# State products on half-array tiles: 128x64 tiles side by side in place of one full-array product

## The chip, the cores and the metric

One core of a Trainium2 chip. The metric is the device time of one execution in microseconds (us). Most executions of one kernel agree within 0.3%; all runs compared below are of the fast state, except row_tiles, a single run whose state is unknown. The word "span" is the profiled execution from its first to its last instruction; it is about 1.8 us shorter than the device time. The "granted clock" is the share of full TensorE speed that the throttle let through; 1.0 is all of it. The "chain of waits" is the chain of work that ended last, followed back from the last instruction to whatever released it.

## The reference

Linear attention without a softmax, then a feed-forward block. Cut to what matters:

```python
# batch 8, heads 8, seq 576, head_dim 64
kv  = np.einsum('bhsd,bhse->bhde', k, v)      # the state: one 64x64 matrix per head  <- this change
out = np.einsum('bhsd,bhde->bhse', q, kv)
out = out / rms(out) * g_norm
x   = out.transpose(0, 2, 1, 3).reshape(4608, 512)
xn  = x / rms(x) * rms_g
y   = (silu(xn @ w_gate) * (xn @ w_val)) @ w_out     # 512 -> 1536 -> 512, nearly all of the work
```

## The kernel before

The kernel runs the feed-forward block of batch n in 12 "up" units (four gate and four value matmuls of 512 columns each) and 4 "down" units, and places the attention work of batch n+1 between them. The state of batch n+1 is made after units 0 and 1 (that of batch 2 after units 2 and 3). Batches 0 and 1 are loaded in another layout and already use 64x64 tiles; batches 2 to 7 take the second half of `kv_pair`, which is what the change touches. There, one matmul serves two heads: 128 columns of weights from k (two heads) and 128 moving columns from v (the same two heads). Its result is a 128x128 block of which only the two 64x64 blocks on the diagonal are used.

```python
    def kv_pair(ps, b, j, first, last):
        if b < EARLY:                      # batches 0 and 1: 64x64 tiles
            ...
            return
        hs = slice(2 * j, 2 * j + 2)
        for t in range(T + 1):             # 5 chunks of rows
            PE.matmul(
                ps, lhsT=bufs[b]["k"][:, t, hs, :], rhs=bufs[b]["v"][:, t, hs, :],
                start=(first and t == 0), stop=(last and t == T),
            )
    ...
        def kv_products(self, js):
            if js[0] == 0:
                self.kv_ps = att_pool.tile([128, NS, 128], FP32, name="att_ps")
            for j in js:
                kv_pair(self.kv_ps[:, j, :], self.n, j, j == 0, j == NS - 1)

        def kv_copy(self):                 # only the diagonal blocks are copied out
            n, ps = self.n, self.kv_ps
            SC.copy(out=kv_all[0:D, n, :, 0:D], in_=ps[0:D, :, 0:D])
            DVE.tensor_copy(out=kv_all[D:128, n, :, D:128], in_=ps[D:128, :, D:128])
    ...
            kv0, os = (2, (4, 5, 7, 8)) if n == 1 else (0, (2, 3, 5, 6))
            if not a.tail:                 # placed after two successive up units
                steps[kv0] += [lambda a=a: a.kv_products((0, 1))]
                steps[kv0 + 1] += [lambda a=a: a.kv_products((2, 3)), a.kv_copy]
            for c, u in enumerate(os):     # first product that reads the state: unit 2
                steps[u].append(lambda a=a, c=c: a.o(c))
```

So there are 12 "groups" of state products (6 batches, two each), every group 10 matmuls between full-array matmuls of 512 columns. One other place uses column tiles already: the products of the sequence tails (`o_products`, line L338), four groups of 8 matmuls of 128x64 weights and 128 moving columns, alternating between the left and the right half of the array.

Of the kernel before, what the change touches and what calls it, by code (L numbers as in the profile page):

```python
# [20 lines left out]
def kernel(  # L21
# [14 lines left out]
    B, H, S, D = q.shape  # L36
# [5 lines left out]
    T = 4  # L42
# [35 lines left out]
    PE, DVE, SC, GP = nc.tensor, nc.vector, nc.scalar, nc.gpsimd  # L78
# [34 lines left out]
    bufs = {b: {"k": kbs[b % 2], "v": vbs[b % 2]} for b in range(B)}  # L113
# [8 lines left out]
    def pairs_buf(b, name):  # L122
        flat = bufs[b][name].rearrange("p t h d -> p (t h d)")
        return flat[:, 0 : NS * C * D].rearrange("p (j c d) -> p j c d", j=NS, c=C)
# [135 lines left out]
    def kv_pair(ps, b, j, first, last):  # L260
        if b < EARLY:
            for c in range(C):
                for u in range(2):
                    rows = slice(u * D, u * D + D)
                    PE.matmul(  # L265
                        ps[rows, rows], lhsT=pairs_buf(b, "k")[rows, j, c, :], rhs=pairs_buf(b, "v")[rows, j, c, :],
                        start=(first and c == 0), stop=(last and c == C - 1),
                    )
            return
        hs = slice(2 * j, 2 * j + 2)  # L270
        for t in range(T + 1):
            PE.matmul(  # L272
                ps, lhsT=bufs[b]["k"][:, t, hs, :], rhs=bufs[b]["v"][:, t, hs, :],
                start=(first and t == 0), stop=(last and t == T),
            )

    def clear_tail_rows(i, engine):

# [12 lines left out]
    class Att:  # L291
# [8 lines left out]
# [5 lines that stand above are left out]
# [345 lines left out]
    def state0(j, dummies):  # L650
        ps = att_pool.tile([128, 512], FP32, name="att_ps")
        warm(ps, max(dummies, 1), 512 if dummies else 128)
        kv_pair(ps[:, 0:128], 0, j, True, True)
        return ps
# [101 lines left out]
    first = ffn.pair_banks()  # L756
# [202 lines left out]
    for n in range(1, B + 1):  # L959
# [25 lines left out]
        b = n + 2  # L985
# [53 lines left out]
```

## Time and profile before

| | before |
|---|---|
| time, median (first runs) | 324.66 us (324.35 to 336.14) |
| span of the profiled run | 322.7 us, granted clock 1.0 |
| TensorE busy | 98% of the span |
| chain of waits | 92% TensorE |
| state products of batches 2 to 7 | 120 matmuls in 12 groups, 0.559 us each, 6.7 us in all |

The page of the kernel before, busy time and chain of waits (time, share of the span, number of instructions; then the shares of the chain by engine; then two groups of instructions, with busy us, mean ns of one, and us idle before them; PE is TensorE's matmuls, PEld its weight loads):

```profile
span 322.7 us, 5143 instructions
...
PE 316.0 (98%) x1925; PEld 156.5 (49%) x1925; DVE 181.5 (56%) x373; ACT 178.3 (55%) x318; POOL 20.3 (6%) x42
...
PE 92%; DMA 4%; DVE 2%; SPq 0%; ACT 0%; issue 0%; DVEq 0%
...
L272 PEld LDWEIGHTS <-kb 128*128 128x128 bf16 x120 | 7.7, 98 | 2.8
L272 PE MATMUL att_ps<-vb,kb 128*128 128x128 bf16 x120 | 8.7, 219 | 0.0
```

A busy share near 100% does not prove a bound by itself, since a matmul's record (219 ns here) is longer than its pace. What proves it is the order in time. Here is TensorE around the two groups of batch 3 (start, time to the last end, instruction, count); only the starts are to be read, since ends overlap:

```profile
90.08 1.03 PE L472 MATMUL v_ps<-xnt,wv_sb 128*128 128x512 bf16 x4
90.94 0.72 PE L272 MATMUL att_ps<-vb,kb 128*128 128x128 bf16 x10
91.50 1.03 PE L472 MATMUL g_ps<-xnt,wg_sb 128*128 128x512 bf16 x4
92.36 1.03 PE L472 MATMUL v_ps<-xnt,wv_sb 128*128 128x512 bf16 x4
93.22 0.72 PE L272 MATMUL att_ps<-vb,kb 128*128 128x128 bf16 x10
```

Four matmuls of 512 columns take 0.86 us wherever they stand (90.08 to 90.94, 91.50 to 92.36), so nothing is lost on either side of a group, and the group takes 91.50 - 90.94 = 0.56 us, 56 ns a matmul. The column-tiled groups that the kernel already has look different:

```profile
258.98 1.03 PE L472 MATMUL v_ps<-xnt,wv_sb 128*128 128x512 bf16 x4
259.94 0.41 PE L338 MATMUL att_ps<-kv_all,qt 128*64 128x128 bf16 x8
260.28 1.04 PE L472 MATMUL g_ps<-xnt,wg_sb 128*128 128x512 bf16 x4
261.15 1.03 PE L472 MATMUL v_ps<-xnt,wv_sb 128*128 128x512 bf16 x4
```

Here the four matmuls ahead of the group take 0.96 us, not 0.86, and the group is longer than its pairs explain. These lines, and the 64x64 groups of batches 0 and 1, are what the prediction is built from.

### The profile page before, as it was taken

The numbers are of one execution on the slowest core, as the hardware profiler recorded it, in microseconds if no ns is written. First come the engines' busy times: TensorE is split into PE (matmuls) and PEld (weight loads), VectorE is DVE, ScalarE is ACT, GpSimd is POOL, SyncE is SP. The second block draws the span as 40 slices with busy tenths as digits, with TensorE's granted clock in tenths as the row PEclk, the third lists the DMA queues.
The fourth block names the chain that finished last, engine by engine and source line by source line (L and its number), as shares of the span: only waits on it lengthen the run. The fifth ranks groups of instructions, "written<-read, shape, count | busy, mean of one in ns | idle before, by whom it ended". The sixth has DMA issues, their size and how long they took to land.

```text
span 322.7 us, 5143 instructions
## 1 busy us (share of the span) xinstructions
PE 316.0 (98%) x1925; PEld 156.5 (49%) x1925; DVE 181.5 (56%) x373; ACT 178.3 (55%) x318; POOL 20.3 (6%) x42
## 2 busy tenths in 40 slices
PE   8899999999999999999999999999999999999995
PEld 3575456554455445544554454445544444444443
DVE  4785767568438922793279417850696068703310
ACT  3576447666757475747664766576554355223321
POOL 1363251100000000000000000000000000000000
PEclk9999999999999999999999999999999999999999
DMA  7999999887379557924792378936102600240014
GB/s 277 355 351 386 377 374 293 214 265 176 65 195 295 132 143 163 328 54 114 187 328 56 73 202 222 315 55 169 43 2 49 182 31 1 48 147 4 0 35 98
DMA packets 74421, 54.87 MB, mean 170 GB/s; under 512 B 42264, under 2 KB 67100, under 8 KB 74396
## 3 DMA queue, kind: packets, MB, share of 16 engines
q1 hardware_dynamic: 74016, 53.88, 58.4%
q10 hardware_dynamic: 380, 0.66, 0.6%
q8 instruction: 15, 0.25, 0.3%
q14 instruction: 10, 0.08, 0.1%
HBM read 37.75 MB, written 9.44 MB: 146 GB/s over the span
## 4 chain that ended last, share of the span: by engine, by line
PE 92%; DMA 4%; DVE 2%; SPq 0%; ACT 0%; issue 0%; DVEq 0%
PE g_ps L472 28%; PE v_ps L472 28%; PE o_ps L516 27%; DMA st<-in_q_dram 3%; PE att_ps L272 2%; PE att_ps L343 2%; PE v_ps L516 1%; PE g_ps L516 1%; DVE xna L453 1%; DMA out_dram<-o_sb 1%; PE v_ps L489 1%; PE o_ps L489 1%; PE g_ps L489 0%; PE att_ps L338 0%; PE att_ps L285 0%; PE att_ps L265 0%
## 5 line engine op out<-in xcount | busy, mean ns | idle before, releaser
L478 DVE TENSOR_TENSOR h_sb<-silu,v_ps 128x512 bf16<-128x512 bf16 x104 | 71.0, 683 | 110.3 <-ACT silu L477 66.9
L472 PE MATMUL g_ps<-xnt,wg_sb 128*128 128x512 bf16 x416 | 106.8, 379 | 0.0
L472 PE MATMUL v_ps<-xnt,wv_sb 128*128 128x512 bf16 x416 | 106.7, 379 | 0.0
L477 ACT ACTIVATE silu<-g_ps 128x512 bf16<-128x512 f32 x104 | 62.5, 601 | 64.4 <-PE g_ps L472 53.7
L516 PE MATMUL o_ps<-wo_sb,h_sb 128*128 128x512 bf16 x396 | 87.4, 379 | 0.0
L472 PEld LDWEIGHTS <-wv_sb 128*128 128x128 bf16 x416 | 40.7, 98 | 49.1
L516 PEld LDWEIGHTS <-h_sb 128*128 128x128 bf16 x420 | 40.7, 98 | 47.7
L472 PEld LDWEIGHTS <-wg_sb 128*128 128x128 bf16 x416 | 38.7, 98 | 40.0 <-issue 0.4
L106 ACT COPY o_sb<-o_ps 128x512 f32<-128x512 f32 (+1 forms) x34 | 19.7, 580 | 38.0 <-PE o_ps L516 37.3
L361 DVE TENSOR_REDUCE ssq<-sq 128x16 f32<-128x1024 bf16 x28 | 34.1, 1219 | 1.0
L352 ACT ACTIVATE sq<-att_ps 128x512 bf16<-128x512 f32 x28 | 16.7, 597 | 13.1 <-PE att_ps L343 8.7
L106 ACT CAST vb<-st 128x512 bf16<-128x512 f32 (+2 forms) x33 | 18.9, 625 | 4.7 <-DMA st<-in_v_dram 4.7
L378 DVE TENSOR_TENSOR xna<-outa,s1y 128x512 bf16<-128x512 bf16 x28 | 17.9, 684 | 0.0
L354 ACT CAST outa<-att_ps 128x512 bf16<-128x512 f32 x28 | 16.2, 579 | 0.0
L106 ACT CAST qb<-st 128x1024 bf16<-128x1024 f32 (+1 forms) x15 | 14.2, 987 | 1.9 <-DMA st<-in_q_dram 1.9
L106 ACT CAST kb<-st 128x512 bf16<-128x512 f32 (+1 forms) x25 | 14.0, 619 | 0.0
L360 DVE TENSOR_TENSOR sq<-sq,gsq 128x512 bf16<-128x512 bf16 x28 | 11.7, 418 | 0.0
L343 PEld LDWEIGHTS <-qt 128*128 128x128 bf16 x96 | 7.4, 98 | 5.7
L343 PE MATMUL att_ps<-kv_all,qt 128*128 128x128 bf16 x96 | 9.3, 219 | 0.0
L272 PEld LDWEIGHTS <-kb 128*128 128x128 bf16 x120 | 7.7, 98 | 2.8
L617 PE MATMUL att_ps<-kv_all 128*128 128x512 bf16 (+1 forms) x21 | 7.6, 490 | 1.2 <-DVE sel L606 1.2
L272 PE MATMUL att_ps<-vb,kb 128*128 128x128 bf16 x120 | 8.7, 219 | 0.0
(141 smaller groups left out, 166.9 us busy)
## 6 DMA issues: line engine op xcount, KB each, us to landing
st<-in_q_dram SPq DMA_DIRECT2D x7, 1024.0 KB, 6.5
out_dram<-o_sb SPq DMA_DIRECT2D x14, 512.0 KB, 3.2
st<-in_k_dram SPq DMA_DIRECT2D x6, 1024.0 KB, 10.2
st<-in_v_dram SPq DMA_DIRECT2D x6, 1024.0 KB, 11.2
st<-in_moe_w_out_dram SPq DMA_DIRECT2D x6, 512.0 KB, 11.4
st<-in_moe_w_gate_dram SPq DMA_DIRECT2D x4, 512.0 KB, 9.4
st<-in_moe_w_val_dram SPq DMA_DIRECT2D x4, 512.0 KB, 9.8
st<-in_k_dram SPq DMA_DIRECT2D x4, 288.0 KB, 4.0
```

What stands on the lines that cost most here:

```text
L106: engine.copy(out=dst, in_=src)
L272: PE.matmul(ps, lhsT=bufs[b]["k"][:, t, hs, :], rhs=bufs[b]["v"][:, t, hs, :], start=(first and t == 0), stop=(last and t == T),)
L343: PE.matmul(cols, lhsT=self.qt[:, j, 128 * c : 128 * c + 128], rhs=kv_all[:, self.n, j, :], start=(j == 0), stop=(j == NS - 1),)
L352: SC.activation(out=self.sq[c][:, 0], in_=ps, func=ACT.Square)
L354: SC.copy(out=self.outa[c], in_=ps)
L360: DVE.tensor_tensor(out=sq[:, 1], in0=sq[:, 0], in1=gsq8, op=OP.mult)
L361: DVE.reduce_sum(out=self.ssq[:, c], in_=sq, axis=AX.X)
L378: DVE.tensor_tensor(out=self.xna[c], in0=self.outa[c], in1=self.alpha[:, c, :].to_broadcast([128, H, D]), op=OP.mult)
L472: PE.matmul(ps, lhsT=wt[:, s, j * 128 : (j + 1) * 128], rhs=x[:, s, :], start=(s == 0), stop=(s == NS - 1),)
L477: SC.activation(out=silu, in_=g_ps, func=ACT.Silu)
L478: DVE.tensor_tensor(out=self.h[:, j, :], in0=silu, in1=v_ps, op=OP.mult)
L516: PE.matmul(self.o_ps[c], lhsT=self.h[:, j, c * 128 : (c + 1) * 128], rhs=wo_sb[:, j, :], start=(j == 0), stop=(j == NF - 1),)
```

## The change

The intent is to stop computing the unused off-diagonal blocks. Each head gets its own matmul of 64 weight columns and 64 moving columns; the output rows 0 to 63 or 64 to 127 place it on the left or the right half of the array, and the two are issued alternately so that they can run side by side. The whole diff:

```diff
-        hs = slice(2 * j, 2 * j + 2)
         for t in range(T + 1):
-            PE.matmul(
-                ps, lhsT=bufs[b]["k"][:, t, hs, :], rhs=bufs[b]["v"][:, t, hs, :],
-                start=(first and t == 0), stop=(last and t == T),
-            )
+            for u in range(2):
+                rows = slice(u * D, u * D + D)
+                PE.matmul(
+                    ps[rows, rows], lhsT=bufs[b]["k"][:, t, 2 * j + u, :], rhs=bufs[b]["v"][:, t, 2 * j + u, :],
+                    start=(first and t == 0), stop=(last and t == T),
+                )
```

The order of all other instructions is the same; lines below move down by one (L272 is L273 after, L472 is L473).

## The prediction

> **What bounds the kernel.** TensorE: PE is busy 98% of the 322.7 us span on the page and 92% of the chain of waits, at full granted clock. From 60 us on it issues without a gap, so its time won or lost shows one for one.
>
> **The changed part now.** Batches 2 to 7 make their state products (L272) in 12 groups of 10 matmuls between full-array 512-column products. The timeline shows 0.559 us a group: a matmul each 56 ns, nothing lost on entry (the first starts 215 ns after the last 512-column one) or exit (56 ns). All 12: 6.7 us, 2% of the time.
>
> **The change.** 120 matmuls of 128 columns become 240 of 64 columns, in pairs on the left and right half of the array; the unused off-diagonal blocks are no longer computed. Only PE gets more instructions (120 loads, 120 matmuls).
>
> Two terms, from this trace:
>
> 1. *Streaming.* The 64x64-tile products of batches 0 and 1 (L265) show a pair of 64-column matmuls on two tiles, with its loads, each 31.7 ns. The tail products (L338), in just this 128x64 tiling, show that two column tiles run together: a pair of 128-column matmuls each 55.5 ns, the pace of one on the whole array. At 31.7 ns a pair, a group saves 10 x (55.9 - 31.7) = 0.242 us.
>
> 2. *Switching.* Around each L338 group time is lost: the first matmul starts 309 ns after the last 512-column one instead of 216 (+93), the second pair 80 ns after the first (+25), the next full-array matmul about 153 ns after the last pair instead of 56 (+97), the one behind it +10: some 0.225 us, the same in all four groups. The Trainium skill, "TensorEngine Tiling (Array Packing)", Key Properties, says that changing the tiling mode drains the TensorE; these gaps agree.
>
> Net: 0.559 to about 0.317 + 0.225 = 0.54 us a group, a gain of 0.02; times 12, 0.2 us. The terms cancel.
>
> **The doubt.** The trace does not settle whether two 128-row, 64-column weight loads run side by side: L338's 55.5 ns a pair would fit two in turn as well. "TensorE: Matmul & The Clock Gate", Part 3, says that loads overlap with running matmuls only when the row group differs; here both tiles use all rows. L338's second loads start 28 ns after its first: a hint of side by side. If they serialise, a pair stays at 55 ns, a group costs 0.78 us, and the change loses 12 x 0.22 = 2.7 us (0.8%). One chance in four.
>
> **Critical path.** All of it: TensorE is gapless around every group. The state copies behind it (ACT, then DVE) end 0.7 us before the first product that reads them, so a slip of 0.1 us there changes nothing.
>
> **Prediction.** 324.7 us, 80% range 323.5 to 327.5. Faster by over 2%: 0.01; within 2%: 0.97; slower by over 2%: 0.02.
>
> **What the profile should show.** The changed line with 240 matmuls of 128x64, some 190 ns each; pairs each 32 ns (55 if loads serialise); about 309 ns into a group and 125 to 150 out; a group of 0.54 us (0.78); the span moved by 12 times the difference; all else unchanged.
>
> **What would make it wrong.** Pairs slower than 55 ns, if a 64-column load of 128 rows blocks the other tile's matmuls (beyond 100 ns a pair the loss passes 6 us); a switch that costs less than at L338.

## The result

324.44 us median (323.89 to 325.03, 6 runs), beside 324.67 us for before (324.23 to 336.14, 6 runs; the 336.14 is a slow run and is left out of the ratio). The ratio is 0.9997, 95% interval 0.9983 to 1.0012. A ratio here is the mean time of one kernel's fast runs over that of the other's of the same rounds, so it is not quite the ratio of the medians. The change is even, as predicted.

The page after:

```profile
span 322.9 us, 5346 instructions
...
PE 312.5 (97%) x2008; PEld 153.7 (48%) x2045; DVE 182.0 (56%) x373; ACT 178.2 (55%) x318; POOL 20.2 (6%) x42
...
PE 87%; DVE 4%; DMA 3%; ACT 2%; issue 2%; another core or an unknown queue 1%; SPq 0%; DVEq 0%; ACTq 0%
...
L473 PE MATMUL g_ps<-xnt,wg_sb 128*128 128x512 bf16 x404 | 106.0, 379 | 0.8 <-ACT wg_sb L201 0.2
L473 PE MATMUL v_ps<-xnt,wv_sb 128*128 128x512 bf16 x402 | 103.9, 379 | 0.1
...
L473 PEld LDWEIGHTS <-wv_sb 128*128 128x128 bf16 x416 | 40.7, 98 | 49.1
...
L273 PEld LDWEIGHTS <-kb 128*64 128x64 bf16 x240 | 4.7, 112 | 5.1 <-issue 5.1
```

Three things here could mislead. TensorE seems 3.5 us less busy, but its matmul records are incomplete: 404 and 402 of the 416 that the weight loads show. The chain's TensorE share falls from 92% to 87%, though nothing new bounds the kernel: the idle time at a change of tiling is booked as "issue", and where a cast happens to end just as a delayed group starts, the chain steps over to ACT. That cast is not the cause, because the second group of every batch, with no cast near it, starts equally late; in batches 3 to 7 no instruction of that second group waits for a semaphore, and its first matmul still starts 309 to 310 ns after the last 512-column one. And the weight loads of the new groups show 5.1 us idle before them, 0.42 us a group; most of that is only the load no longer being issued ahead. The loss is read from matmul starts instead:

```profile
90.56 1.03 PE L473 MATMUL v_ps<-xnt,wv_sb 128*128 128x512 bf16 x4
91.52 0.51 PE L273 MATMUL att_ps<-vb,kb 128*64 128x64 bf16 x20
91.95 1.04 PE L473 MATMUL g_ps<-xnt,wg_sb 128*128 128x512 bf16 x4
92.83 1.03 PE L473 MATMUL v_ps<-xnt,wv_sb 128*128 128x512 bf16 x4
93.78 0.51 PE L273 MATMUL att_ps<-vb,kb 128*64 128x64 bf16 x20
```

From one value product to the next, before: 0.86 + 0.56 + 0.86 = 2.28 us (90.08 to 92.36). After: 0.96 + 0.43 + 0.88 = 2.27 us (90.56 to 92.83). The group is 0.13 us shorter, and its two borders take back 0.10 + 0.02. With the single records of that group, in ns:

| | before | after |
|---|---|---|
| last 512-column start to the group's first | 215 | 309 |
| first pair to second pair (before: two matmuls) | 112 | 52 |
| each further pair (before: two matmuls) | 112 | 31.7 |
| group's first start to the next 512-column start | 559 | 437 |
| that one to the one behind it | 216 | 226 |
| sum of rows 1, 4 and 5 | 990 | 972 |

So a group gains 18 ns, and 12 of them 0.22 us. In terms of the prediction: a pair costs 31.7 ns, so ten save 559 - 317 = 242 ns; the switch costs 94 on entry, 20 on the second pair, 99 on the way out and 10 behind it, 223 ns.

A gain of 0.2 us is below what the timed runs resolve. But the traces resolve it, because the kernel is periodic from batch 4 on. I use the *batch period*: the start of the first state product's weight load of batch 7 minus that of batch 4, over three. Before it is (223.08 - 123.81) / 3 = 33.090 us, after it (223.74 - 124.57) / 3 = 33.057 us. The difference is 0.033 us a batch, for two groups of 0.018. Starts are printed to 0.01 us, so a period in the table below is good to about 0.003 us. The packed traces hold them to the nanosecond: there the periods are 33.090 and 33.056.

### The profile page after: what moved, and what is told of

The parts are those of the page before. It is cut to its first block, busy times and chain, and to the rows that moved or that the text cites. A ratio compares the mean times of both kernels' runs of the same rounds, so it can differ in the third digit from the quotient of the medians.

```text
span 322.9 us, 5346 instructions
## 1 busy us (share of the span) xinstructions
PE 312.5 (97%) x2008; PEld 153.7 (48%) x2045; DVE 182.0 (56%) x373; ACT 178.2 (55%) x318; POOL 20.2 (6%) x42
## 4 chain that ended last, share of the span: by engine, by line
PE 87%; DVE 4%; DMA 3%; ACT 2%; issue 2%; another core or an unknown queue 1%; SPq 0%; DVEq 0%; ACTq 0%
PE g_ps L473 26%; PE o_ps L517 26%; PE v_ps L473 26%; PE att_ps L344 2%; PE att_ps L273 2%; DMA st<-in_v_dram 2%; ACT vb L106 1%; DMA st<-in_k_dram 1%; PE v_ps L517 1%; PE g_ps L517 1%; DVE xna L454 1%; DVE ssq L362 1%; PE att_ps L265 1%; DMA out_dram<-o_sb 1%
## 5 line engine op out<-in xcount | busy, mean ns | idle before, releaser
L473 PE MATMUL g_ps<-xnt,wg_sb 128*128 128x512 bf16 x404 | 106.0, 379 | 0.8 <-ACT wg_sb L201 0.2
L473 PE MATMUL v_ps<-xnt,wv_sb 128*128 128x512 bf16 x402 | 103.9, 379 | 0.1
L473 PEld LDWEIGHTS <-wv_sb 128*128 128x128 bf16 x416 | 40.7, 98 | 49.1
L473 PEld LDWEIGHTS <-wg_sb 128*128 128x128 bf16 x416 | 38.3, 98 | 40.4 <-issue 0.3
L618 PE MATMUL att_ps<-kv_all 128*128 128x512 bf16 (+1 forms) x19 | 6.9, 496 | 1.2 <-DVE sel L607 1.2
L108 DVE CAST kb<-st 128x576 bf16<-128x576 f32 (+1 forms) x12 | 5.9, 516 | 2.7 <-DMA st<-in_k_dram 2.6
L273 PEld LDWEIGHTS <-kb 128*64 128x64 bf16 x240 | 4.7, 112 | 5.1 <-issue 5.1
```

The lines of the kernel that those rows point to most:

```text
L273: PE.matmul(ps[rows, rows], lhsT=bufs[b]["k"][:, t, 2 * j + u, :], rhs=bufs[b]["v"][:, t, 2 * j + u, :], start=(first and t == 0), stop=(l ...
L473: PE.matmul(ps, lhsT=wt[:, s, j * 128 : (j + 1) * 128], rhs=x[:, s, :], start=(s == 0), stop=(s == NS - 1),)
```

## The experiments

The theory: the change is even because two terms cancel, on the critical path, in full: ten pairs save 0.242 us and one switch in and out costs 0.223. Rivals: (1) time in this stage is hidden, so that nothing done there shows; (2) the gap at a group's border belongs to the semaphore waits at its start, not to the tiling; (3) pairs cost as much as before and the switch nothing, which would be even as well. All results, with the two kernels for reference; "us" is (ratio - 1) x 324.5 against before:

| run | groups | ratio to before (95%) | us | batch period, us |
|---|---|---|---|---|
| before | 12 | | | 33.090 |
| after | 12 | 0.9997 (0.9983 to 1.0012) | -0.1 | 33.057 |
| after_merged | 6 | 0.9955 (0.9937 to 0.9973) | -1.5 | 32.830 |
| before_merged | 6 | 1.0001 (0.9982 to 1.0020) | 0.0 | 33.090 |
| after_split | 24 | 1.0118 (1.0093 to 1.0142) | +3.8 | 33.617 |
| before_split | 24 | 1.0047 (1.0026 to 1.0069) | +1.5 | 33.303 |
| after_split3 | 18 | 1.0039 (1.0017 to 1.0061) | +1.3 | 33.280 |
| before_split3 | 18 | 1.0010 (0.9981 to 1.0040) | +0.3 | 33.090 |
| before_double | 12 | 1.0205 (1.0175 to 1.0234) | +6.7 | 34.207 |
| after_double | 12 | 1.0156 (1.0129 to 1.0182) | +5.1 | 33.687 |
| after_double_late | 12 | 1.0089 (1.0072 to 1.0105) | +2.9 | 33.687 |
| after_inturn | 12 | 1.0029 (1.0007 to 1.0052) | +0.9 | 33.167 |
| row_tiles (wrong result) | 12 | one run, 327.31 us | +3.1 | 33.513 |
| merged_tail | 6 | 0.9940 (0.9925 to 0.9955) | -1.9 | 32.831 |

All but row_tiles gave the right result. The `after_` kernels are edits of the changed kernel, the `before_` ones the same edit of the kernel before.

### The switch: fewer of them

```diff
-                steps[kv0] += [lambda a=a: a.kv_products((0, 1))]
-                steps[kv0 + 1] += [lambda a=a: a.kv_products((2, 3)), a.kv_copy]
+                steps[kv0 + 1] += [lambda a=a: a.kv_products((0, 1, 2, 3)), a.kv_copy]
```

> The changed kernel with both groups of a batch issued as one: 6 groups of 20 pairs in place of 12 of 10. Theory (about 31.7 ns a pair, plus about 0.225 us for each entry and exit of the column tiling, all on the critical path): six switches fewer, each worth 0.225 us, so 1.3 to 1.4 us less than the changed kernel (323.1 us against 324.4), ratio to before about 0.995; each group takes 0.437 + 10 x 0.0317 = 0.754 us from its first matmul to the next full-array one, with 309 ns ahead of it. Rival 1 (the change is even because TensorE time of this stage is hidden behind other work): no change, ratio 0.9995 to 1.000. Rival 2 (the gap belongs to the waits on semaphores at a group's start, not to the tiling): the control before_merged gains as much.

> Control: the kernel before with the same merging. Theory: no switch to save, so ratio to before 0.999 to 1.001 and 20 matmuls in 20 x 56 = 1.12 us with 216 ns in and 56 ns out. Rival 2 (gap from the semaphores at a group's start): gains like after_merged.

Measured: 323.18 us and 324.65 us, before 324.55 in the same rounds. TensorE in after_merged, batch 3:

```profile
91.33 1.03 PE L473 MATMUL v_ps<-xnt,wv_sb 128*128 128x512 bf16 x4
92.29 0.82 PE L273 MATMUL att_ps<-vb,kb 128*64 128x64 bf16 x40
93.04 1.04 PE L473 MATMUL g_ps<-xnt,wg_sb 128*128 128x512 bf16 x3
93.92 1.03 PE L473 MATMUL v_ps<-xnt,wv_sb 128*128 128x512 bf16 x4
```

The entry is again 0.96 us and the group 0.75 us, as expected (the "x3" is a missing record: the next product starts 0.88 us later, as behind any group). The batch period falls by 33.057 - 32.830 = 0.227 us, one switch, and the whole by 1.4 us for six. The control does not move (33.090), so rivals 1 and 2 fall: time here is in the open, and groups on the whole array cost nothing to begin. The tiled second groups without any semaphore wait, above, speak against rival 2 as well.

### The switch: more of them

The edit, cut to its new lines; `middle` is called between the gate and the value products of a unit:

```diff
+                steps[kv0] += [lambda a=a: a.kv_products((0,))]
+                middle[kv0 + 1] = [lambda a=a: a.kv_products((1,))]     # between gate and value products
+                steps[kv0 + 1] += [lambda a=a: a.kv_products((2,))]
+                middle[kv0 + 2] = [lambda a=a: a.kv_products((3,)), a.kv_copy]
```

> The changed kernel with each pair of heads a group of its own (24 groups of 5 pairs, placed between the gate and the value products of the units). Theory: 12 more switches at 0.225 us, so 2.7 us more than the changed kernel: about 327.1 us, ratio to before about 1.008; groups of 0.437 - 5 x 0.0317 = 0.28 us with 309 ns ahead. Rival 1 (hidden): no change. If a switch costs in proportion to the work around it, less than 2.7 us.

> Control of after_split on the kernel before: same 24 groups, all on the whole array. Theory: ratio to before 0.999 to 1.001, entries 216 ns and exits 56 ns. Rival 2: 2.7 us slower like after_split.

Measured: 328.31 us and 326.13 us, before 324.55. The control failed: on the whole array, too, splitting cost 1.5 us. TensorE and VectorE of before_split show why (batch 4):

```profile
129.27 1.03 PE L472 MATMUL v_ps<-xnt,wv_sb 128*128 128x512 bf16 x4
130.34 0.38 PE L343 MATMUL att_ps<-kv_all,qt 128*128 128x128 bf16 x4
```

```profile
129.86 0.43 DVE L309 CAST kv_all<-att_ps 64x256 bf16<-64x256 f32 x1 [1.06 <-ACT kv_all L308]
```

The last group now comes half a unit later, and the first product that reads the state (L343) waits for the state copy, which ends at 130.29; it starts 1.07 us after the value products instead of 0.86. That is 0.21 us a batch, which the control's period shows in full (33.303 - 33.090). My split had cost a wait of its own, so the times of this pair tell nothing clean of the switch; the records of after_split do show the expected 309 ns in and 0.28 us a group. It was repeated with 18 groups, the last group and the copies where they belong:

```diff
+                steps[kv0] += [lambda a=a: a.kv_products((0,))]
+                middle[kv0 + 1] = [lambda a=a: a.kv_products((1,))]
+                steps[kv0 + 1] += [lambda a=a: a.kv_products((2, 3)), a.kv_copy]
```

> The splits of the first call put the last group so late that the first q product then waited for the state copies (the control lost 0.21 us a batch to that). Here 18 groups (5, 5 and 10 pairs), the last one and the copies where the changed kernel has them. Theory: 6 switches more than the changed kernel at 0.225 us, so 1.3 to 1.4 us more than it, 325.8 us beside 324.5 for before, ratio about 1.0035. Rival 1 (hidden): ratio 0.9995.

> Control of after_split3 on the whole array, copies in place. Theory: ratio to before 0.999 to 1.001. If it is slower as before_split was (1.0047), splitting itself costs and the copy wait was not the reason.

Measured: 325.70 us and 324.62 us, before 324.56. The control's period is that of before; the tiled version's is 33.280 - 33.057 = 0.223 us longer, one switch a batch. (From the nanosecond starts, merging and splitting both give 0.225.) The switch is the same 0.22 us ahead of 5, 10 or 20 pairs.

### The pairs: twice as many

The edit, cut to what matters:

```diff
-            for j in js:
-                kv_pair(self.kv_ps[:, j, :], self.n, j, j == 0, j == NS - 1)
+            for again in range(2):     # batches 2 to 7 only
+                for j in js:
+                    kv_pair(self.kv_ps[:, j, :], self.n, j, j == 0 and again == 0, j == NS - 1 and again == 1)
```

> The kernel before with every state product issued twice into the same accumulation (states twice as large; the normalisation that follows divides that out, so the result stays right). Theory: 120 more matmuls of the whole array at 56 ns, all on the critical path: 6.7 us more, ratio to before 1.0205. Rival 1 (this stage is hidden): no change.

> The same doubling of the changed kernel: 120 more pairs at 31.7 ns and no more switches: 3.8 us more than the changed kernel, ratio to before about 1.011, so 2.9 us less than before_double + its own 0.2 us: about 3.1 us. Rival (a pair costs 56 ns and a switch nothing, which would leave the change even as well): as slow as before_double.

Measured: 331.43 us and 329.70 us. The control is as expected: 20 more matmuls a batch lengthen the period by 34.207 - 33.090 = 1.117 us, 55.9 ns each. The tiled period grows by 33.687 - 33.057 = 0.630 us, 31.5 ns a pair (31.7 from the nanosecond starts), which rules out rival 3. But the whole came out 5.3 us above the changed kernel by the medians, not 3.8. The trace of after_double has one wait of TensorE that the others lack (columns: us in total, times, longest):

```profile
PE g_ps L478 <- DMA xnt<-xna: 0.9, 1, 0.9
PE g_ps L478 <- issue: 0.2, 1, 0.2
```

It falls at 89.8 us, where the feed-forward block of batch 2 begins and needs its activations through four transposing DMAs. The Sync engine's timeline has them in after_double and, for comparison, in before_double:

```profile
83.53 6.17 SPq L391 DMA_TRANSPOSE xnt<-xna  x4
90.20 0.37 SPq L545 DMA_DIRECT2D out_dram<-o_sb  x1
```

```profile
84.06 5.16 SPq L390 DMA_TRANSPOSE xnt<-xna  x4
89.72 0.38 SPq L544 DMA_DIRECT2D out_dram<-o_sb  x1
```

They take 1.0 us longer, all of it in the first, whose issue took 2.24 us (1.22 in the other traces). In that stretch (83.4 to 86 us of after_double) one instruction fetch ran, at 84.1 us:

```profile
q1 hardware_dynamic: 503, 0.13, 31.7%
q8 instruction: 1, 0.02, 2.9%
```

In the other traces, the fetches of this queue fall elsewhere (70.5 and 92.7 us in the changed kernel). More TensorE instructions move these fetches (there are 15 in before, 16 in after, 18 in after_double), and here one may have hit a DMA whose slack is nil. To test that, batch 2 was left undoubled:

```diff
-            if self.n < EARLY:
+            if self.n <= EARLY:        # EARLY = 2
```

> after_double came out 5.3 us above the changed kernel in place of 3.8, though its batches 3 to 7 took just the 0.63 us more each that 31.7 ns a pair gives. In its trace TensorE waits 1.1 us once, at 89.8 us, for a transposing DMA of batch 2 whose issue took 2.2 us in place of 1.2, while a 16 KB instruction fetch ran. Here batch 2 is not doubled (160 TensorE instructions fewer before that point), so that fetch moves away. Theory: no such wait, 5 x 0.634 = 3.2 us above the changed kernel, 327.6 us, ratio to before about 1.009. Rival (doubling costs 5.3 us by itself): about 5/6 of it, 4.4 us, 328.8 us.

Measured: 327.18 us, ratio 1.0089. The four DMAs take 5.15 us again, TensorE shows no wait between 60 and 120 us, the period is the same 33.687, and the fetch is at 92.2 us. In us against before, 2.9 + 0.1 = 3.0 stands against the expected 3.2 and the rival's 4.4. So the surplus of after_double is a one-off delay and not a cost of pairs. The edit also moved everything else by a fraction of a us, so this run alone does not show that the fetch caused the delay. The packed traces of all 14 runs go further. They hold 784 transposing DMAs. The 37 that ran for at least 0.4 us alongside a fetch of queue q8 took 1.65 to 2.53 us each; the 11 with a shorter overlap took 1.22 to 1.31. Of the 736 that met no such fetch, 721 took 1.19 to 1.47 us and 15 took longer, 14 of these being one DMA at 59 us of every run. So a fetch alongside went with a slow issue every time, but no run moved a fetch and nothing else.

### Do the tiles need to alternate?

```diff
-        for t in range(T + 1):
-            for u in range(2):
-                rows = slice(u * D, u * D + D)
+        for u in range(2):
+            rows = slice(u * D, u * D + D)
+            for t in range(T + 1):
```

> The changed kernel with the two tiles' matmuls no longer alternating: for each pair of heads five on the left tile, then five on the right. Theory (a pair costs 31.7 ns only because neighbours in the queue use different tiles; matmuls start in order, and one tile takes a new one each 32 ns at best): some 32 ns a matmul, 0.64 us a group more or less in place of 0.32, 12 x 0.32 = 3.8 us more than the changed kernel, about 328.2 us, ratio to before 1.011. Rival (the array finds the parallel work by itself, within its queue): no change. If weight loads of the same tile cannot go ahead of its running matmul, worse than 3.8 us.

Measured: 325.19 us, before 324.21. My expectation was wrong. TensorE, batch 3:

```profile
90.46 1.03 PE L473 MATMUL v_ps<-xnt,wv_sb 128*128 128x512 bf16 x4
91.42 0.56 PE L273 MATMUL att_ps<-vb,kb 128*64 128x64 bf16 x20
91.91 1.04 PE L473 MATMUL g_ps<-xnt,wg_sb 128*128 128x512 bf16 x4
```

A group takes 0.49 us in place of 0.44, not 0.75: the period grows by 0.110 us, 0.055 a group, 0.7 us in all. The starts of the single matmuls, in ns from the first, explain it; the first record on each tile is the longer one (217 ns, the others 196), which marks where the right tile begins:

```
one series    0    53    84   116   148   179 ...
the other    58   111   143   174   206 ...
```

Two series of ten run side by side, each a matmul every 32 ns once it is going. The second begins at 58 ns, although all five of the left tile's matmuls (0 to 148 ns) stand ahead of it in the program. All 20 start within 364 ns; one tile at 32 ns each would have needed over 600. A second mark agrees: the program built from this kernel holds five left, then five right, and of these ten, in batch 3, only the first and the fifth of the left tile wait for a semaphore. The trace has the second of these waits at 148 ns, behind three matmuls of the right tile (58, 111 and 143 ns). Matmuls of different tiles therefore overtake each other in the queue. Alternating is better, but only by the 55 ns that the second tile starts late.

### Is it column tiles, or any change of tiling?

The edit against the kernel before, without the lines that allot the second bank:

```diff
-            PE.matmul(
-                ps, lhsT=bufs[b]["k"][:, t, hs, :], rhs=bufs[b]["v"][:, t, hs, :],
+            for u in range(2):
+                rows = slice(u * D, u * D + D)
+                PE.matmul(
+                    (ps, other)[u], lhsT=bufs[b]["k"][rows, t, hs, :], rhs=bufs[b]["v"][rows, t, hs, :],
```

> Wrong result on purpose (half of the rows' sum goes to a bank that nobody reads). The kernel before with each state product as two row tiles, 64 rows by all 128 columns, 128 columns streamed: does the switch cost belong to any change of tiling or to column tiles alone? If to any: 309 ns into each of the 12 groups and some 150 ns out, pairs each 56 ns, about 2.7 us above before. If to column tiles alone: 216 ns in, 56 out, time as before.

Measured: 327.31 us in one run. TensorE, batch 3:

```profile
90.87 1.03 PE L475 MATMUL v_ps<-xnt,wv_sb 128*128 128x512 bf16 x4
91.83 0.73 PE L274 MATMUL att_ps<-vb,kb 64*128 64x128 bf16 x20
92.50 1.04 PE L475 MATMUL g_ps<-xnt,wg_sb 128*128 128x512 bf16 x4
93.37 1.03 PE L475 MATMUL v_ps<-xnt,wv_sb 128*128 128x512 bf16 x4
```

The entry is 0.96 us again (311 ns from start to start, 309 with column tiles), the exit 148 ns behind the last matmul, and pairs of 128 columns take 56 ns. The period is 33.513 - 33.090 = 0.423 us longer, 0.21 a group. So the switch belongs to row tiles as much as to column tiles. (The one timed run, 3.1 us above before, is of unknown state; the reading rests on the trace.)

### A better version

Fewer switches is the lesson, and the tail products have four of them. Issued two by two, into two banks:

```diff
         def o(self, c):
-            ps = att_pool.tile([128, H, D], FP32, name="att_ps")
-            self.o_products(c, ps)
+            if self.tail:
+                if c % 2 == 0:
+                    self.o_pair(c)          # products of c and c + 1, one group of 16
+                ps = self.o_ps[c]
+            else:
+                ps = att_pool.tile([128, H, D], FP32, name="att_ps")
+                self.o_products(c, ps)
```

> Candidate for best: after_merged, and the four groups of tail products (also 128x64 tiles) issued as two groups of 8 pairs into two banks. Theory: two switches fewer, 2 x 0.225 = 0.45 us below after_merged, so about 322.7 us, ratio to before about 0.994. If the earlier second product delays something else by holding both banks, less or nothing.

Measured: 322.27 us, before 324.21 in the same rounds; ratio 0.9940 (0.9925 to 0.9955). It beats both kernels, by 0.6% of before. Against after_merged (0.9955) the step is 0.0015, 0.5 us, as expected, though those two intervals overlap. The trace is clearer: a group of 16 lasts 0.570 us, first start to the next full-array start, where two of 8 lasted 0.347 each, and with one entry fewer that makes 0.23 us a merged pair of groups.

## Why the prediction was right

The measured 324.44 us stands beside 324.7 predicted, within 323.5 to 327.5. But a forecast of "no change" is right easily, so the steps matter more.

- **TensorE is gapless, so time here counts in full.** Shown: every switch and every pair added or removed came back in the batch period, and in the whole as far as timing resolves it (after_double had its one delayed DMA on top).
- **Streaming.** Predicted 31.7 ns a pair, from the 64x64 tiles; measured 31.7 in the records and 31.5 (31.7 unrounded) from doubling. A saving of 0.242 us a group, as predicted.
- **Switching.** Predicted 0.225 us from the tail products; measured 0.223 from the records, 0.227 from merging and 0.223 from splitting (0.225 for both, unrounded). The second pair cost +20 ns rather than +25, the exit +99 rather than +97.
- **Net.** Predicted 0.2 us less; 0.22 us by the records, below what timing resolves.
- **The doubt.** Whether the two tiles' weight loads run side by side got one chance in four of costing 2.7 us. They do: a pair took 31.7 ns, not the 55 of the doubt, and in the packed trace the two loads of a pair start 3 to 4 ns apart and the next two some 30 ns later. The sentence of the Trainium skill, "TensorE: Matmul & The Clock Gate", Part 3, on which the doubt rested, does not hold here; "TensorEngine Tiling (Array Packing)", Key Properties, which says that different tiles can load weights and multiply in parallel, does. The trace of the kernel before could have said as much of the sentence: its full-array weight loads start 54 ns before their matmul, while the one before, on the same rows, is under way.
- **The drain.** The same Key Properties say that changing the tiling mode drains the TensorE, and changing the tile alone does not. The traces agree: each visit, one change in and one out, costs 0.22 us with column tiles and 0.21 with row tiles, and no such gap stands between tiles of one mode. They show the gaps; that a drain fills them is the page's reading.

Where expectations failed was in the experiments: the in-turn order (0.7 us by the traces, not 3.8), the first split (a wait for the state copies that I had made myself), and after_double (one delayed DMA).

## What to carry to other kernels

Packing two small products side by side in the array saves a fixed amount for each pair and costs a fixed amount for each visit to the tiling mode (the same ahead of 5, 10 and 20 pairs here). Here a pair saved 24 ns and a visit cost 0.22 us, so a group breaks even at 223 / 24.2, some nine pairs, and ten gained too little for timed runs to show. So gather tiled work into few long groups before tiling it: the same change with half the visits was worth 0.45%. Read such costs from start to start on either side of a group, not from busy time.

## What the Trainium skill lacked or had wrong

- "TensorEngine Tiling (Array Packing)", Key Properties, says that a mode switch drains the TensorE but gives no figure. Here one visit between 512-column matmuls at full clock costs 0.22 us: 94 ns in, 20 ns on the second pair, 99 ns out, 10 ns behind; 0.21 us with 64x128 row tiles.
- "TensorE: Matmul & The Clock Gate", Part 3, says in its list of what overlaps that weight loads overlap running matmuls only when the row group differs (its paragraph on the mechanism also names loads into the background weight buffer). With two tiles that share all 128 rows, pairs with both loads took 31.7 ns, against 55.9 ns for one full-array matmul of 128 columns.
- The same part says that matmuls start strictly in program order. With the tiles issued five and five, 20 matmuls started within 364 ns in two interleaved series of 32 ns, and the left tile's fifth started behind the right tile's third: matmuls of different tiles overtake. The trace does not show the order in which they end, so the page's advice of one semaphore increment on the last matmul is not tested here.
- I found no page that links instruction fetches to delayed DMA issues. In one trace a transposing DMA took 2.24 us to issue instead of 1.22 while a fetch ran, and TensorE lost about 1 us; over all 14 traces, each of the 37 that ran at least 0.4 us alongside a q8 fetch took 1.65 to 2.53 us. That the fetch is the cause is likely; no run moved it alone.
